# Mirrored token pairs in a fused FFT and MLP kernel: shared first layer in row tiles, maxima on VectorE, output sums on GpSimd, mirrored rows loaded by SyncE

**Chip, cores, metric.** One core of one Trainium2 chip. The metric is device time in microseconds (us) of one execution, lower is better. A profiled execution's *span* (first to last instruction) is about 2 us shorter than its time.

## The reference, cut to what matters

```python
# x: (8, 3136, 256) float32; U: (3136, 32); V: (32, 3136); w_ch1: (256, 1024); w_ch2: (1024, 256)
X  = np.fft.fft(np.fft.fft(x, axis=1), axis=2).real          # over the sequence, then over the features
h  = X.transpose(0, 2, 1) @ U @ V                            # low-rank mixing along the sequence
u  = X + h.transpose(0, 2, 1)
out = u + np.maximum(u @ w_ch1, 0.0) @ w_ch2                 # a two-layer MLP per token, with its residual
```

The 3136 tokens are treated as 49 "lines" of 64. The real part of the transform has a symmetry: token k and its mirror share the even half of the transformed row and have opposite odd halves. The kernel before uses it for the transform; the change uses it for the MLP too.

## The kernel before: the parts that matter

Batches are handled in four pairs. While one pair goes through the MLP, the rows of the next pair are loaded, folded and transformed by work placed between the MLP's slots. A chunk load, and the folds that use it:

```python
def load_pair_chunk(p, c):
    ...
    nc.sync.dma_start(out=ck.xa[:, 0:4, :], in_=x_pn[r0:r0 + PR, 4 * c + 1:4 * c + 5, :])      # PR = 98 rows
    ...
    nc.gpsimd.indirect_dma_start(                                                              # mirrored rows
        out=ck.xb.rearrange("p l d -> p (l d)"), out_offset=None, in_=x_g,
        in_offset=bass.IndirectOffsetOnAxis(ap=idx[:, 8 * p + c:8 * p + c + 1], axis=0))

def fold_d(yb, src, l0, l1):                         # after GpSimd has added xa and the reversed xb into y
    o, i = yb[:, l0:l1, :], src[:, l0:l1, :]
    nc.vector.tensor_tensor(o[:, :, 1:128], i[:, :, 1:128], i[:, :, 255:128:-1], op=AL.add)
    nc.vector.tensor_tensor(o[:, :, 129:256], i[:, :, 1:128], i[:, :, 255:128:-1], op=AL.subtract)
    nc.vector.tensor_copy(o[:, :, 0:129:128], i[:, :, 0:129:128])
```

The MLP: TensorE at full height, relu on ScalarE, output sums on VectorE, stores on SyncE.

```python
def mlp1(ch, jp):
    ...
    for i in range(2):
        ...
        for blk in range(2):
            nc.tensor.matmul(ps[:, i, 0:n], (W1p if ch.sg > 0 else W1m)[jp // 2][:, blk, j],
                             q[:, blk, c0:c0 + n], start=(blk == 0), stop=(blk == 1))
    nc.scalar.activation(ch.h[:, 2 * jp:2 * jp + 2, 0:n], ps[:, :, 0:n], AF.Relu)

def mlp2(ch, t, last=False):
    ...
    for j in range(JT):                              # JT = 8
        nc.tensor.matmul(ps, ch.h[:, j, t * P:(t + 1) * P], W2[:, j, :], ...)
        if j < 2:
            nc.tensor.matmul(ps[:, j], q[:, j, tk], (Bp if ch.sg > 0 else Bm)[:, j], ...)       # residual
    ...
    def drain():
        ...
        nc.scalar.copy(om[:, 0:n], ch.po[:, 0:n, 1])
        nc.vector.tensor_tensor(ob[:, 0:n, 0:P], ch.po[:, 0:n, 0], om[:, 0:n], op=AL.add)
        nc.vector.tensor_tensor(ob[:, 0:n, P:D], ch.po[:, 0:n, 0], om[:, 0:n], op=AL.subtract)
        ...                                          # nc.sync.dma_start of each half of ob
```

Of the kernel before, what the change touches and what calls it, by code (L numbers as in the profile page):

```python
# [22 lines left out]
def kernel(  # L23
# [21 lines left out]
    x_g = x.rearrange("b (n1 g l) d -> (b n1 g) (l d)", g=16, l=4)  # L45

    cpool = ctx.enter_context(tc.tile_pool(name="cpool", bufs=1))
    xpool = ctx.enter_context(tc.tile_pool(name="xpool", bufs=4))
# [3 lines left out]
    qpool = [ctx.enter_context(tc.tile_pool(name="qpool0", bufs=1)), None]  # L52
# [4 lines left out]
    T = cpool.tile([P, NK1, P], BF16)  # L57
# [3 lines left out]
    W1m = [cpool.tile([P, 2, 512], BF16, name=f"W1m{c}") for c in range(2)]  # L61
    W2 = cpool.tile([P, JT, D], BF16)
    Bp = cpool.tile([P, 2, P], FP16)
    Bm = cpool.tile([P, 2, P], FP16)
    tes = [cpool.tile([P, D], BF16, name=f"te_{b}") for b in range(2)]
    idx = cpool.tile([PR, 8 * NP], I32)
# [22 lines left out]
    def load_pair_chunk(p, c):  # L89

        ck = Obj()
        ck.c = c
        r0 = p * PR
        ck.xa = xpool.tile([PR, 5, D], FP32, tag="xa", name="xa")
        ck.xb = xpool.tile([PR, 4, D], FP32, tag="xb", name="xb")
        nc.sync.dma_start(out=ck.xa[:, 0:4, :], in_=x_pn[r0:r0 + PR, 4 * c + 1:4 * c + 5, :])
        if c == 7:
            nc.sync.dma_start(out=ck.xa[:, 4, :], in_=x_pn[r0:r0 + PR, 0, :])
        nc.gpsimd.indirect_dma_start(  # L99
            out=ck.xb.rearrange("p l d -> p (l d)"), out_offset=None, in_=x_g,  # L100
            in_offset=bass.IndirectOffsetOnAxis(ap=idx[:, 8 * p + c:8 * p + c + 1], axis=0))
        return ck

    def load_single(b):
# [10 lines left out]
        if b == 0:  # L115
            first.q = qpool[0].tile([P, 2, 6272], BF16, tag="q", name="q")
            xl = first.q[0:1].rearrange("p a j -> p (a j)")[:, 0:32 * D].rearrange("p (l d) -> p l d", d=D)
            nc.gpsimd.dma_start(out=xl, in_=x_pn[r0 + L:r0 + N1, 0:32, :])
        rows(33, 1, X[1:2 * L:2, 0:31, :])
        if b == 0:  # L120
            yield
            nc.sync.dma_start(out=X[PR - 2:PR - 1, 31::-1, :], in_=xl)
            yield
        else:
            nc.gpsimd.dma_start(out=X[PR - 2:PR - 1, 31::-1, :], in_=x_pn[r0 + L:r0 + N1, 0:32, :])
            yield
# [5 lines left out]
    def fold_d(yb, src, l0, l1):  # L132
# [3 lines left out]
        nc.vector.tensor_copy(o[:, :, 0:129:128], i[:, :, 0:129:128])  # L136
# [19 lines left out]
    class Pair:  # L156
        def __init__(self, p):
            self.p, self.z, self.q = p, None, None
# [10 lines left out]
    def s1_steps(pr, evac):  # L169
# [5 lines left out]
        def step(g):  # L175
            yb, l = pr.chunks[g // 2].yb, 2 * (g % 2)
            ps = psd.tile([P, 2, D], FP32, tag="ps", name="ps")
            if g == 15:
                parts = [(ps[:, 0], yb[:, 4], 1), (ps[:, 0], yb[:, 3], 2), (ps[:, 1], yb[:, 2], 0)]
            else:  # L180
                parts = [(ps[:], yb[:, l:l + 2], 0)]
# [6 lines left out]
            evac(z[:, 31::-31, :] if g == 15 else z[:, 30 - 2 * g:28 - 2 * g:-1, :] if g < 14 else z[:, 2:0:-1, :], ps[:])  # L188
            if g % 4 == 3:
                lo = max(30 - 2 * g - 1, 0)  # L190
                hi = 37 - 2 * g
                nc.scalar.dma_start(out=zdp[:, lo:hi, :], in_=z[:, lo:hi, :])
                if g == 15:
                    nc.scalar.dma_start(out=zdp[:, 31, :], in_=z[:, 31, :])
# [4 lines left out]
    def line32(b, ps=None, start=True):  # L199
        ps = ps if ps is not None else psd.tile([P, 2, D], FP32, tag="ps", name="ps32")  # L200
# [59 lines left out]
    def turn(pr, b, parts, engines=(nc.sync,)):  # L260
        g = gpool.tile([P, NK1, D], BF16, tag=f"g{b}", name="g")
        src = zd[pr.p % 2, b].rearrange("k cn d -> cn k d")
        for i, (k0, k1) in enumerate(parts):
            engines[i % len(engines)].dma_start(out=g[0:64, k0:k1], in_=src[:, k0:k1, :])
        pr.g[b] = g

    def te_out(pr, b, ps, c0, s0, spread):
        te = tes[b]
        nc.vector.tensor_copy(te[64:96, 0:129], ps[c0:c0 + 32, 0, 0:129])
        nc.vector.tensor_copy(te[96:128, 129:256], ps[s0:s0 + 32, 0, 129:256])  # L270
        spread(pr.g[b], te)

    def te_steps(pr, spread):
# [4 lines left out]
        def step(lo, hi):  # L278
            if lo == 0:
                st.ps = psd.tile([P, 2, D], FP32, tag="ps", name="teps")  # L280
# [5 lines left out]
            if hi == 32:  # L286
                for b in range(2):
                    te_out(pr, b, st.ps, 32 * b, 64 + 32 * b, spread)

        for lo, hi in [(0, 20), (20, 32)]:  # L290
            yield lambda lo=lo, hi=hi: step(lo, hi)

    def te_single(pr, b, spread, ps=None):

        ps = ps or psd.tile([P, 2, D], FP32, tag="ps", name="teps")
# [4 lines left out]
        te_out(pr, b, ps, 0, 32, spread)  # L300

    def spread(parts):
        def run(g, te):
            src = te[64:128].bitcast(I32)
            for eng, k0, k1 in parts:
                eng.tensor_copy(g[64:128, k0:k1].bitcast(I32), src.unsqueeze(1).to_broadcast([64, k1 - k0, D // 2]))  # L306
        return run

    def two(row, a, b, n):

        v = row[:, a:a + n]
        return bass.AP(row.tensor, v.offset, [list(v.ap[0]), [b - a, 2], [1, n]])

    def s3_steps(pr, b, evac):

        if pr.q is None:
            pr.q = qpool[pr.p % 2].tile([P, 2, 6272], BF16, tag="q", name="q")

        def mm(o, k1, blk, st, rows=P, low=None):
            lt = low[:, blk::2] if low is not None else pr.g[b][0:rows, k1, blk::2]  # L320
            r = T[0:rows, k1, 0:64] if k1 == 0 else T[0:rows, k1, :].rearrange("p (s j) -> p s j", s=2)
            nc.tensor.matmul(o, lt, r, start=st, stop=True, skip_group_check=True)  # L322

        def lines(ps, g, blk, rows, low=None):
            for u in range(4):
                us = slice(u * 64, (u + 1) * 64)
                mm(ps[:, 0, us] if 4 * g + u == 0 else ps[:, :, us], 4 * g + u, blk, u == 0 and low is None, rows, low)

        def step(g, blk):
            ps = psd.tile([P, 2, 256], FP32, tag="ps", name="ps")  # L330
            lines(ps, g, blk, P)
            move(ps, g, blk, evac)

        def move_part(ps, g, blk, evac, part):
            lo = 64 if part and g == 0 else 0
            c0 = 3200 + b * 1536 + (4 * g - 1) * 64 if part else b * 1600 + 4 * g * 64
            evac(pr.q[:, blk, c0 + lo:c0 + 256], ps[:, part, lo:256])

        def move(ps, g, blk, evac):
            if g == 0:  # L340
                move_part(ps, g, blk, evac, 0)
                move_part(ps, g, blk, evac, 1)
            else:
                k0 = 4 * g
                evac(two(pr.q[:, blk, :], b * 1600 + k0 * 64, 3200 + b * 1536 + (k0 - 1) * 64, 256), ps[:])

        def last():
            ps = psd.tile([P, 2, 2, 64], FP32, tag="ps", name="ps")
            k1 = NK1 - 1
            for blk in range(2):  # L350
                mm(ps[:, blk], k1, blk, blk == 0)
            for blk in range(2):
                evac(two(pr.q[:, blk, :], b * 1600 + k1 * 64, 3200 + b * 1536 + (k1 - 1) * 64, 64), ps[:, blk])

        yield lines, move_part
        for g in range(6):
            for blk in range(2):
                yield lambda g=g, blk=blk: step(g, blk)
        yield last


    def pair_chunks(p):

        res = []
        plus = [(2 * p + b, k1) for b in range(2) for k1 in range(NK1)]
        minus = [(2 * p + b, N1 - k1) for b in range(2) for k1 in range(1, NK1)]
        for sg, us, lo, hi, base in [(1, plus, 0, 24, 0), (-1, minus, 0, 24, 3200),
                                     (1, plus, 24, 50, 0), (-1, minus, 24, 48, 3200)]:
            for i in range(lo, hi, 8):
                ch = Obj()  # L370
                ch.p, ch.sg, ch.c0, ch.units = p, sg, base + 64 * i, us[i:min(i + 8, hi)]
                res.append(ch)
        return res

    def mlp1(ch, jp):
        q, c0, n = ch.pr.q, ch.c0, 64 * len(ch.units)
        if jp == 0:
            ch.h = hpool.tile([P, JT, 512], BF16, tag="h", name="hT")
        ps = psh.tile([P, 2, 512], FP32, tag="h", name="hps")
        for i in range(2):  # L380
            j = slice((2 * (jp % 2) + i) * P, (2 * (jp % 2) + i + 1) * P)
            for blk in range(2):
                nc.tensor.matmul(ps[:, i, 0:n], (W1p if ch.sg > 0 else W1m)[jp // 2][:, blk, j], q[:, blk, c0:c0 + n],  # L383
                                 start=(blk == 0), stop=(blk == 1))
        nc.scalar.activation(ch.h[:, 2 * jp:2 * jp + 2, 0:n], ps[:, :, 0:n], AF.Relu)  # L385

    def mlp2(ch, t, last=False):
        q, nt = ch.pr.q, len(ch.units) // 2
        if t % 2 == 0 or last:
            ch.po = pso.tile([P, 2, 2, P], FP32, tag="o", name="ops")  # L390
        ps = ch.po[:, 0 if last else t % 2]
        tk = slice(ch.c0 + t * P, ch.c0 + (t + 1) * P)
        for j in range(JT):
            nc.tensor.matmul(ps, ch.h[:, j, t * P:(t + 1) * P], W2[:, j, :],  # L394
# [475 lines left out]
```

## Time and profile before

| | before |
|---|---|
| median of 3 runs (lowest to highest) | 453.54 us (451.29 to 454.5) |
| span of the profiled run, mean granted TensorE clock | 449.6 us, 1.00 |
| busy: TensorE, ScalarE, VectorE, GpSimd | 95%, 65%, 50%, 32% |

The prediction below shows the busy shares, the last chain, the stretches and single instructions. The page's slices: each digit is a fortieth of the span, TensorE's busy share in tenths (9 is 90% or more).

```profile
PE   3889997999999999999999999999999999999995
...
PEclk9999999999999999999999999999999999999999
```

TensorE is full from the eighth slice on, and in this run its clock is never reduced while it works (other runs of the same kernel list a mean of 0.990 to 1.00). From the groups of instructions (count, then busy us and mean ns, then idle time before; the waits list us in total, times, longest): the folding add on VectorE.

```profile
L134 DVE TENSOR_TENSOR yb<-y 98x508 bf16<-98x508 f32 (+1 forms) x24 | 21.1, 879 | 0.1
```

### The profile page before, as it was taken

How to read it: one execution, taken by the hardware profiler on the slowest of the kernel's cores; microseconds unless marked ns; L12 is line 12 of the kernel's file. 1: busy time of each engine (PE TensorE's matmuls, PEld its weight loads, DVE VectorE, ACT ScalarE, POOL GpSimd, SP SyncE). 2: the span in 40 equal slices, each digit the busy share in tenths (PEclk: the TensorE clock that was granted, in tenths of full speed). 3: DMA queues.
4: the chain of work that ended last, by engine and by line, in shares of the span. 5: the costliest groups of instructions: out<-in, count | busy, mean ns of one | idle time of the engine just before them, and what ended most of it. 6: DMA issues, size and time to landing. Idle time of an engine off the chain costs nothing.

```text
span 449.6 us, 10536 instructions
## 1 busy us (share of the span) xinstructions
PE 426.6 (95%) x4158; PEld 308.7 (69%) x4221; DVE 224.6 (50%) x541; ACT 290.3 (65%) x402; POOL 142.6 (32%) x180
## 2 busy tenths in 40 slices
PE   3889997999999999999999999999999999999995
PEld 1756665776777777767867777777867777667764
DVE  7873686874344466373354467363354344222222
ACT  5886754676565567777465667777466655666662
POOL 7465455851330545550510545360500000000000
PEclk9999999999999999999999999999999999999999
DMA  8749753875592657863772647773662222222323
GB/s 149 159 138 168 211 162 109 254 181 176 162 231 66 171 137 214 235 207 96 171 195 62 171 113 238 223 200 101 165 141 66 71 65 66 72 72 74 85 54 93
DMA packets 59761, 64.34 MB, mean 143 GB/s; under 512 B 12950, under 2 KB 52672, under 8 KB 59552
## 3 DMA queue, kind: packets, MB, share of 16 engines
q1 hardware_dynamic: 50000, 42.68, 36.8%
q0 software_dynamic: 7232, 14.30, 13.5%
q10 hardware_dynamic: 2480, 6.69, 4.0%
q8 instruction: 33, 0.54, 0.5%
q14 instruction: 16, 0.13, 0.1%
HBM read 34.62 MB, written 32.19 MB: 149 GB/s over the span
## 4 chain that ended last, share of the span: by engine, by line
PE 84%; DVE 5%; DMA 3%; issue 3%; POOL 2%; ACT 1%; SPq 1%; DVEq 0%; ACTq 0%; POOLq 0%
PE ops L394 35%; PE hps L383 35%; PE ps L322 5%; PE ops L397 4%; PE ps L185 2%; DMA out_dram<-ob 2%; PE teps L284 1%; DMA w_f<-in_moe_w_ch_dram 1%; SPq L412 1%; DVE g L76 1%; ACT hT L385 1%; PE w1ps L679 1%; DVE q L76 0%; DVE ta L447 0%; DVE ob L407 0%
## 5 line engine op out<-in xcount | busy, mean ns | idle before, releaser
L385 ACT ACTIVATE hT<-hps 128x1024 bf16<-128x1024 f32 (+1 forms) x208 | 202.6, 976 | 109.6 <-PE hps L383 100.9
L394 PE MATMUL ops<-W,hT 128*128 128x256 bf16 x1568 | 224.7, 273 | 1.2 <-DVE ob L408 1.0
L394 PEld LDWEIGHTS <-hT 128*128 128x128 bf16 x1568 | 145.1, 98 | 35.0 <-DVE ob L408 0.8
L76 DVE CAST q<-ps 128x512 bf16<-128x512 f32 (+3 forms) x121 | 65.2, 560 | 83.8 <-PE ps L322 80.1
L383 PE MATMUL hps<-q,W1p 128*128 128x512 bf16 (+1 forms) x420 | 103.2, 355 | 2.6 <-DVE q L76 0.5
L407 DVE TENSOR_TENSOR ob<-ops,om 128x256 f32<-128x256 f32 (+1 forms) x102 | 41.8, 410 | 117.7 <-ACT om L406 116.3
L383 PE MATMUL hps<-q,W1m 128*128 128x512 bf16 x351 | 95.7, 379 | 2.1 <-ACT hT L385 0.5
L144 POOL TENSOR_TENSOR y<-xa,xb 98x510 f32<-98x510 f32 (+1 forms) x48 | 60.9, 1289 | 108.5 <-DMA xa<-in_x_dram 84.2
L383 PEld LDWEIGHTS <-W1p 128*128 128x128 bf16 x448 | 40.3, 98 | 27.3 <-issue 2.2
L383 PEld LDWEIGHTS <-W1m 128*128 128x128 bf16 x384 | 35.3, 98 | 26.5 <-issue 1.4
L397 PEld LDWEIGHTS <-q 128*128 128x128 bf16 x392 | 38.3, 98 | 21.6 <-issue 0.9
L406 ACT COPY om<-ops 128x256 f32<-128x256 f32 (+1 forms) x102 | 37.3, 366 | 14.4 <-PE ops L394 7.8
L306 POOL COPY g<-te 64x1024 int32<-64x1024 int32 (+1 forms) x23 | 24.9, 1122 | 56.3 <-DVE te L270 51.7
L408 DVE TENSOR_TENSOR ob<-ops,om 128x256 f32<-128x256 f32 (+1 forms) x102 | 41.2, 404 | 0.0
L73 ACT CAST z<-ps 128x512 bf16<-128x512 f32 x48 | 28.2, 587 | 17.2 <-PE ps L185 16.4
L397 PE MATMUL ops<-Bp,q 128*128 128x128 f16 x200 | 38.4, 219 | 0.0
L322 PE MATMUL ps<-T,g 128*128 128x128 bf16 (+3 forms) x400 | 36.9, 218 | 0.5 <-ACT q L73 0.3
L397 PE MATMUL ops<-Bm,q 128*128 128x128 f16 x192 | 36.9, 219 | 0.0
L322 PEld LDWEIGHTS <-g 128*128 128x128 bf16 (+1 forms) x400 | 29.4, 98 | 5.0 <-issue 0.6
L99 POOL DMA_INDIRECT xb<-in_x_dram,idx x24 | 25.1, 1044 | 5.4 <-issue 4.5
L134 DVE TENSOR_TENSOR yb<-y 98x508 bf16<-98x508 f32 (+1 forms) x24 | 21.1, 879 | 0.1
L76 DVE COPY g<-zt 32x400 bf16<-32x400 bf16 (+3 forms) x45 | 17.2, 383 | 6.3 <-ACT zt L73 5.7
(136 smaller groups left out, 208.1 us busy)
## 6 DMA issues: line engine op xcount, KB each, us to landing
out_dram<-ob SPq DMA_DIRECT2D x389, 64.0 KB
xa<-in_x_dram SPq DMA_DIRECT2D x24, 392.0 KB
zturn<-z ACTq DMA_DIRECT2D x9, 512.0 KB
g<-zturn SPq DMA_DIRECT2D x3, 800.0 KB
g<-zturn SPq DMA_DIRECT2D x3, 544.0 KB
X<-in_x_dram POOLq DMA_DIRECT2D x4, 384.0 KB, 7.7
X<-in_x_dram POOLq DMA_DIRECT2D x2, 744.0 KB
zturn<-z ACTq DMA_DIRECT2D x3, 448.0 KB
```

The lines of the kernel that those rows point to most:

```text
L73: nc.scalar.copy(o, i)
L76: nc.vector.tensor_copy(o, i)
L99: nc.gpsimd.indirect_dma_start(out=ck.xb.rearrange("p l d -> p (l d)"), out_offset=None, in_=x_g, in_offset=bass.IndirectOffsetOnAxis(ap=i ...
L144: nc.gpsimd.tensor_tensor(ck.y[:, l0:l1, 1:256], ck.xa[:, l0:l1, 1:256], rb[:, l0:l1, 255:0:-1], op=AL.add)
L322: nc.tensor.matmul(o, lt, r, start=st, stop=True, skip_group_check=True)
L383: nc.tensor.matmul(ps[:, i, 0:n], (W1p if ch.sg > 0 else W1m)[jp // 2][:, blk, j], q[:, blk, c0:c0 + n], start=(blk == 0), stop=(blk == 1))
L385: nc.scalar.activation(ch.h[:, 2 * jp:2 * jp + 2, 0:n], ps[:, :, 0:n], AF.Relu)
L394: nc.tensor.matmul(ps, ch.h[:, j, t * P:(t + 1) * P], W2[:, j, :], start=(j == 0 and (t % 2 == 0 or last)), stop=(j == JT - 1), skip_group ...
L397: nc.tensor.matmul(ps[:, j], q[:, j, tk], (Bp if ch.sg > 0 else Bm)[:, j], start=False, stop=False, skip_group_check=True)
L406: nc.scalar.copy(om[:, 0:n], ch.po[:, 0:n, 1])
L407: nc.vector.tensor_tensor(ob[:, 0:n, 0:P], ch.po[:, 0:n, 0], om[:, 0:n], op=AL.add)
L408: nc.vector.tensor_tensor(ob[:, 0:n, P:D], ch.po[:, 0:n, 0], om[:, 0:n], op=AL.subtract)
```

## The change

The intent is to let the first layer be computed once for the two tokens of a mirrored pair. With a and b the even and odd parts, relu(a+b) = max(a, -b) + b and relu(a-b) = max(a, b) - b; the b terms are linear and go through the product W1·W2 into the residual weights. Even and odd parts lie on 64 rows each, so that TensorE works on two row tiles at a time. ScalarE copies the odd part out of PSUM, VectorE forms both maxima with the even part read from PSUM, GpSimd forms the output sums, `te` (the transformed tokens times U, the inner part of the low-rank mixing) is no longer spread over the rows of `g` (the transformed lines from which the MLP's input is made), and the mirrored rows are loaded by SyncE in two groups of 49. The diff, cut to its core:

```diff
-        nc.gpsimd.indirect_dma_start(
-            out=ck.xb.rearrange("p l d -> p (l d)"), out_offset=None, in_=x_g,
-            in_offset=bass.IndirectOffsetOnAxis(ap=idx[:, 8 * p + c:8 * p + c + 1], axis=0))
+        r = 2 * p * N1 * 16 + 48 * 16 + 15 - c
+        nc.sync.dma_start(out=ck.xb.rearrange("p l d -> p (l d)"),
+                          in_=bass.AP(x.tensor, x.offset + r * 4 * D, [[N1 * 64 * D, 2], [-64 * D, N1], [1, 4 * D]]))
 ... (fold_d)
-        nc.vector.tensor_copy(o[:, :, 0:129:128], i[:, :, 0:129:128])
+        nc.scalar.copy(o[:, :, 0:129:128], i[:, :, 0:129:128])
 ... (first layer)
-        nc.scalar.activation(ch.h[:, 2 * jp:2 * jp + 2, 0:n], ps[:, :, 0:n], AF.Relu)
+                for s in range(2):                                   # row tiles 0..63 (even) and 64..127 (odd)
+                    lt = W1z[64:P, ja] if s and blk == 0 else W1p[c][64 * s:64 * s + 64, blk, jc]
+                    nc.tensor.matmul(o[s], lt, q[64 * s:64 * s + 64, blk, c0:c0 + w], ...)
+ ...                                                                 # the te part: TE by VZ, 33 rows per tile
+        ab = apool.tile([P, 512], BF16, tag="ab", bufs=3, name="ab")
+        nc.scalar.copy(ab[:], ps[:, 1])
+        ...
+        nc.vector.scalar_tensor_tensor(h[:, 1], b, -1.0, a, op0=AL.mult, op1=AL.max)
+            nc.vector.tensor_tensor(flip[0][:, :, ::-1], flip[1], flip[2], op=AL.max)
 ... (second layer: two phases; phase 1 waits for a no-op on ScalarE that follows phase 0)
+            for j in range(JT):
+                for s, op, half in sides:
+                    mm = nc.tensor.matmul(op, ch.h[rows[half], s, j, t * P:(t + 1) * P], W2[rows[half], j, :], ...)
+                    if ha and j == 0 and half == 0:
+                        tc.add_manual_dep(mm.ins, st.turn.ins.name, sync, reason="bank turn")
+            if ha == 0:
+                st.turn = nc.scalar.nop()
 ... (drain; eng is GpSimd except at the very end)
+                nc.scalar.copy(om, po)
+            eng.tensor_tensor(ob[:, 0:n, 0:P], a, om[:, :, 1], op=AL.add)
+            eng.tensor_tensor(ob[:, 0:n, P:D], a, om[:, :, 1], op=AL.subtract)
 ... (te row of each group of lines; the turn of z through DRAM moves from ScalarE's queue to SyncE's)
+            nc.sync.dma_start(out=zr, in_=q[64:65, 0, c0:c0 + 512])
-                nc.scalar.dma_start(out=zdp[:, lo:hi, :], in_=z[:, lo:hi, :])
+                nc.sync.dma_start(out=zdp[:, lo:hi, :], in_=z[:, lo:hi, :])
 ... (placing of the next pair's steps)
-                for o, f in [(0, load), (4, fn), (7, fd), (9, s1[2 * c]), (10, s1[2 * c + 1])]:
+                for o, f in [(0, load), (2, fn), (4, fd), (5, s1[2 * c]), (5, s1[2 * c + 1])]:
```

A slot of the kernel before is a quarter of a chunk of 512 tokens, one of the changed kernel half a chunk of 256 mirrored pairs, so that "slot" in the last lines has different lengths (1.8 and 3.5 us of TensorE work). The cut leaves out that the loaded rows have three buffers instead of four; b1 below keeps four.

## The prediction, on record before anything of the change was built

> **What bounds the kernel now.** I read the shares of the page first, then the chain of work that ended last, then the waits, then busy time by stretches and single instructions of TensorE in order of time.
>
> ```profile
> PE 426.6 (95%) x4158; PEld 308.7 (69%) x4221; DVE 224.6 (50%) x541; ACT 290.3 (65%) x402; POOL 142.6 (32%) x180
> ...
> PE 84%; DVE 5%; DMA 3%; issue 3%; POOL 2%; ACT 1%; SPq 1%; DVEq 0%; ACTq 0%; POOLq 0%
> ```
>
> TensorE is busy for 95% and is 84% of the last chain. No other engine passes 65%. The stretches (columns: length, then PE, PEld, DVE, ACT, POOL busy) say that this is a full engine, not one that waits in pieces:
>
> ```profile
> 70.00:80.00 10.00, 7.69 (x100) 5.50 (x101) 6.91 (x21) 4.23 (x7) 5.32 (x6) 1.00 0.36 90
> ...
> 130.00:140.00 10.00, 9.95 (x98) 7.67 (x97) 6.21 (x13) 5.87 (x7) 0.00 (x0) 1.00 0.42 125
> 200.00:210.00 10.00, 9.95 (x77) 7.04 (x77) 4.03 (x12) 7.80 (x11) 0.00 (x0) 1.00 0.40 120
> ...
> 440.00:450.00 10.00, 4.46 (x43) 3.38 (x40) 2.71 (x10) 1.75 (x6) 0.00 (x0) 0.98 0.38 98
> ```
>
> From 80 us to the end PE holds 9.6 to 9.95 of every 10 us. Losses lie only in the first 28 us (preparation), at 55 to 85 us (about 3 us, in the first pair of batches), and some 5 us at the end. The hole near 70 us is one link of the chain in time:
>
> ```profile
> 68.30 1.22 POOL y L144
> 69.52 0.20 POOL y L145
> 69.72 4.59 issue
> 74.31 1.15 POOL g L306
> ```
>
> GpSimd sits 4.59 us ahead of the copy that spreads `te` over the rows of `g`; PE matmuls on `g` follow it. So the time can fall by much only if TensorE gets less to do.
>
> To count that work I need the spacing of matmuls, not their busy durations, which overlap. The timeline gives it:
>
> ```profile
> 25.20 1.01 PE L322 MATMUL ps<-T,g 64*128 64x64 bf16 x16
> ...
> 114.97 1.32 PE L284 MATMUL teps<-z,UZ 128*64 128x129 bf16 x40
> 116.23 0.40 PE L383 MATMUL hps<-q,W1p 128*128 128x128 bf16 x4
> ...
> 116.79 0.82 PE L394 MATMUL ops<-W,hT 128*128 128x256 bf16 x6
> ```
>
> The last line: six matmuls of 256 columns in 0.82 us, the last lasting 0.27, so 0.55/5 = **0.109 us per 256 columns**; 512 columns take 0.216, 128 take 0.055, single starts show. The first line has 64 contraction rows and costs (1.01-0.22)/15 = 0.053: half the rows alone save nothing. The second has two column tiles: 20 pairs of about 128 columns in 1.10 us, 0.055 per *pair*, so two tiles truly run side by side. It also shows a price: its first start is 0.20 us after the preceding one instead of 0.109, and the first start after it is 0.15 late instead of 0.055, so **about 0.1 us to enter and 0.1 us to leave** a tiling.
>
> [...] 98x510 takes GpSimd 1.317 us, 98x508 takes VectorE 0.926 and 0.857.
>
> **The change, part by part.** Tokens k and 49-k share the even and odd half of the transformed row. The first layer computes both halves once (a and b, 64 contraction rows each, in two row tiles) and forms relu(a+b)=max(a,-b)+b and relu(a-b)=max(a,b)-b; the b terms go linearly through W1·W2 into the residual. One slot is 256 tokens.
>
> *TensorE.* First layer before, per 512 tokens: 16 x 0.216 = 3.46 us; second with its residual 4 x (8 x 0.109 + 2 x 0.055) = 3.93; together 7.38, and 12.25 such per pair of batches = 90.5 us. After, per slot: first layer two times 6 row pairs (four of weights, two of the separate te part) = 1.31; second layer two phases of 8 row pairs and 2 residual pairs = 20 x 0.109 = 2.18; sum 3.49, and 24 slots = 83.7, plus a short chunk of the zero lines of about 2.7: 86.4. Lines (L322): before 100 matmuls x 0.055 = 5.5; after the same number with 64 columns, in row pairs, at most 50 x 0.055 = 2.7. New: te through W1 (8 x 0.216 = 1.7) and through the residual (0.7). Sum: 90.5+5.5 = 96.0 against 91.5, **4.5 us less per pair of batches**. But all is row-tiled now, so the full-height pieces (s1 in eight slots, te) each enter and leave: about 11 more round trips of 0.2 = 2.3 us where a next pair is prepared (three of four). TensorE work: -(3 x 2.2 + 4) = **about -10 us**.
>
> *ScalarE.* Leaves: 202.6 (relu) + 37.3 + 28.2 + 3.9 of 290.3, so 18 stays. Comes: odd halves 192+8 copies 128x512 at 0.587 (z's row) = 117; reversed q 48 x 0.58 = 28; output copies 96 x 0.59 = 57; lines 24 x 1.03 = 25; z 23; te, tables, fold copies 28. About 296 us: same load.
>
> *VectorE.* Leaves: q casts 65 and sums 83, some small: about 60 stays, folding 43 of it. Comes: two maxima per 128x512, at 0.155 + 512 x 1.03 ns = 0.685 (slope from 0.289 at 128 columns to 0.420 at 256, L407): 400 x 0.685 = 274. About **335 us, from 50% to 75% or more**, 82 us of the 98 of a folding pair.
>
> *GpSimd.* Leaves: spread 25, indirect issues 25. Comes: 192 sums of 128x256 at about 0.83 (0.34 at 98x4, 1.317 at 98x510) = 159, small folds 8: about 260 us. No longer idle, not the bound. Loads of mirrored rows move to SyncE's queue: the same bytes, and DMA is at a third; I count nothing.
>
> *Waits.* Before, separate PSUM buffers let PE run ahead. Now four share one ring, and phase 1 must wait for the no-op that stands in ScalarE's line behind the odd copy, in even slots also the reversed q (0.58), and the evacuations of the slot before. In an even slot after a 1.0 us evacuation: lines end 0.55, first layer 1.20, phase 0 2.29, next layer 2.94 us, when PE wants phase 1; ScalarE: evacuation 0.75 to 1.75, output copy to 2.34, odd copy to 2.93, q to 3.51, no-op. PE loses 0.6 us. Some 8 such slots and a few doubled ones: up to 6.5 us per pair, 25 in all.
>
> *Sum.* 453.5 - 10 (matmuls) - 5 (the te hole and its neighbours; no spread is left) + 3 (W1·W2, more tables and evacuations in the first slots) + 6 (waits, a quarter of the worst since the steps seem placed against them) = **447 us**. The quarter is a choice, not a measurement.
>
> **Rivals.** *A, the waits hit in full*: 25 us instead of 6, and VectorE, which in the first pair also has the `g<-zt` copies (17 us over two batches), makes PE stop there: about 466. For it: VectorE over 80% with bursts (a fold is 1.8 us in a 4 us slot), in-order queues, four buffers. Against: ScalarE keeps its 65% and catches up in light slots. *B, the waits are hidden and lines and switches cost less*: tile switches overlap, row-tiled weight loads too; 4.5 x 4 saved, 5 from the hole, no waits: about 430. For it: a schedule this elaborate looks placed by traces. *C, row tiles do not overlap*: a slot's 40 pairs-members run singly, near 7 us instead of 3.5; over 700 us. Nothing in the trace supports it, as column tiles overlap. I give it 2%.
>
> **Range and chances.** Between B and A: 428 to 470. The 2% marks are 444.5 and 462.6. My middle lies just inside "same", but work of TensorE does go and the hole is real, so faster gets 0.42, same 0.34, slower 0.24.
>
> **What would show it.** Right: hT maxima on VectorE near 0.69 us each, VectorE near 335 us; row pairs 0 to 5 ns apart and 0.109 us per pair; PE still the top of the chain with its slices at 8 to 9 rather than a flat 9; waits of PE on ScalarE (no-op, evacuations) of 5 to 10 us in total, and on VectorE maxima a few us. Wrong: a pair spacing well over 0.109 (weight loads in the way), VectorE or GpSimd in the chain for more than a tenth (rival A), or PE flat at 9.9 with a span near 430 (B).

## More of the kernel before

```profile
POOL y L144 <- DMA xa<-in_x_dram: 84.2, 10, 24.7
...
POOL y L144 <- DMA xb<-in_x_dram,idx: 1.4, 1, 1.4
```

GpSimd waited 84 us for `xa`, and no wait of TensorE goes back to that; `xb` was the last to come only once, for 1.4 us. (A wait for several things is put down to the one that came last.)

## The result, and the profile after

| | before | after |
|---|---|---|
| median of 4 runs (lowest to highest) | 452.68 us (451.29 to 454.5) | 616.42 us (612.87 to 617.76) |
| ratio to before, 95% interval | | 1.360 (1.352 to 1.368) |
| span of the profiled run, mean granted clock | 449.6 us, 1.00 | 614.3 us, 0.875 |

Ratios here and below are the mean time of one kernel's fast runs over that of the other's of the same rounds, so not quite the ratio of the medians quoted. The outputs are correct. The change is 36% slower, far outside the range of 428 to 470 us; "slower" was given 0.24.

The page of the changed kernel: busy time, slices, chain.

```profile
PE 485.0 (79%) x8159; PEld 384.2 (63%) x8159; DVE 356.6 (58%) x592; ACT 279.0 (45%) x505; POOL 249.4 (41%) x342
...
PE   4788798294869798886584979878677498999995
...
PEclk9788997686978798797795879988869589999998
...
PE 15%; DVE 3%; ACT 1%; issue 1%; DMA 0%; DVEq 0%; ACTq 0%; POOL 0%
```

Three readings. No engine is a new bound: VectorE holds 58%, the others less. TensorE has holes all through the first 80% of the span and is full only in the last slices, the last pair, in which no next pair is prepared. And **its clock is reduced** in more than half of the slices, which the profile before does not show once. (The chain is of little use here: it goes back only to 482 us of 614.)

**A budget.** I split both spans into TensorE's tail after its last instruction, its idle time, and its busy time, and divided the busy time by the granted clock: stretches on record at half clock are counted half as work, the other half as loss.

| us | before | after | difference |
|---|---|---|---|
| TensorE idle | 18.2 | 122.7 | +104.5 |
| lost to half clock while busy | 0 | 54.8 | +54.8 |
| TensorE work at full clock | 426.6 | 430.2 | +3.6 |
| tail | 4.9 | 6.5 | +1.6 |

(18.2 + 0 + 426.6 + 4.9 = 449.7, and 122.7 + 54.8 + 430.2 + 6.5 = 614.2.) 159 of the 165 us are idle time and half clock. The row of work needs care: a matmul of 256 columns that is followed at once by another adds 0.109 us, but the last one before a pause shows its whole 0.27 us. Pauses over 0.1 us number 16 before and 94 after; an estimate from the matmul records puts what they add to the row at 2.7 and 14.4 us, so that without it the work fell by some 8 us, from 423.9 to 415.9.

**Where it lies in time.** By the first instruction of each pair's MLP:

| length, us | start | pair 0 | pair 1 | pair 2 | pair 3 |
|---|---|---|---|---|---|
| before | 28.0 | 114.0 | 102.1 | 102.2 | 103.4 |
| after | 33.3 | 168.4 | 153.5 | 154.0 | 105.0 |

The last pair, beside which no next pair is prepared, is 1.6 us longer than before. Nearly all, 158 of 165 us, is lost where the next pair is loaded, folded and transformed meanwhile.

**One pause followed back.** Waits of the changed kernel, for the engines that belong to it:

```profile
POOL y L151 <- DMA xb<-in_x_dram: 184.1, 22, 15.0
...
ACT yb L143 <- POOL y L152: 76.9, 18, 11.2
...
DVE yb L141 <- POOL y L151: 62.6, 18, 9.7
...
PE ops L480 <- ACTq L492: 41.3, 11, 8.7
...
PE hps L432 <- DMA VZ<-q: 27.1, 5, 11.6
```

GpSimd, which had waited 86 us for `xa` and `xb` together, now waits 184 us for `xb`, and this time others wait for GpSimd. The timeline (start, busy time; in brackets the idle time before and what ended it) has one such wait from end to end:

```profile
480.55 1.95 POOL L151 TENSOR_TENSOR y<-xa,xb 98x510 f32<-98x510 f32 x2 [15.00 <-DMA xb<-in_x_dram]
...
482.53 3.27 DVE L141 TENSOR_TENSOR yb<-y 98x381 bf16<-98x381 f32 x1 [9.73 <-POOL y L151]
482.69 0.22 ACT L143 CAST yb<-y 98x6 bf16<-98x6 f32 x1 [11.21 <-POOL y L152]
...
482.98 1.89 PE L480 MATMUL ops<-W,hT 64*128 64x256 bf16 x16 [8.66 <-ACTq L492]
```

`xb` lands at 480.5. GpSimd has stood 15 us at its addition; the fold follows; ScalarE has stood 11 us at its small fold copy (L143); behind that copy in its line, at 482.90, stands the no-op between the two phases of the second layer, and TensorE resumes 0.3 us after the copy has begun, 8.66 us idle. The first thing to explain is why `xb` is late, although the same bytes are loaded.

**What the pauses do to the clock.** Stretches of 5 us (busy time of PE, PEld, DVE, ACT, POOL; granted clock; DMA share; GB/s):

```profile
325.00:330.00 5.00, 0.74 (x8) 0.56 (x10) 1.18 (x1) 1.02 (x4) 3.16 (x5) 0.50 0.12 38
330.00:335.00 5.00, 3.29 (x25) 1.71 (x21) 5.00 (x6) 0.73 (x2) 3.67 (x5) 0.50 0.34 78
335.00:340.00 5.00, 4.49 (x46) 3.08 (x47) 3.56 (x6) 2.18 (x4) 1.41 (x2) 0.50 0.38 84
340.00:345.00 5.00, 5.00 (x113) 4.27 (x111) 1.29 (x2) 1.70 (x5) 0.00 (x0) 0.90 0.47 159
```

TensorE is nearly idle from 325 to 330; the clock is at 0.5 and stays there to about 341, long after TensorE is working again: 46 matmuls in 5 us at half clock, 113 at nearly full. All 12 pauses of this trace that are over 2.5 us were followed by half clock, for 3.4 to 17.1 us, so each of these was paid twice.

**What the prediction had right.** From the groups:

```profile
L438 DVE SCALAR_TENSOR_TENSOR hT<-ab,hps 128x512 bf16<-128x512 bf16 x200 | 136.6, 683 | 172.3 <-ACT ab L435 172.2
...
L441 DVE TENSOR_TENSOR hT<-hps,ab 128x512 bf16<-128x512 f32 x192 | 130.8, 681 | 0.0
...
L141 DVE TENSOR_TENSOR yb<-y 98x508 bf16<-98x508 f32 (+1 forms) x24 | 33.8, 1409 | 62.7 <-POOL y L151 62.6
```

The maxima take 0.68 us each, as worked out; the folding add went from 0.88 to 1.41 us, which was not. And from the timeline of the undisturbed last pair:

```profile
565.98 1.03 PE L480 MATMUL ops<-W,hT 64*128 64x256 bf16 x16
...
567.73 1.03 PE L480 MATMUL ops<-W,hT 64*128 64x256 bf16 x16
```

16 matmuls (8 row pairs) in 1.03 us, the members of a pair 0 to 3 ns apart, 0.109 per pair in the mean; phases 1.75 us apart, so 3.50 us a slot, against 3.49 predicted.

### The profile page after: what moved, and what is told of

The parts are those of the page before. It is cut to its first block, busy times and chain, and to the rows that moved or that the text cites. A ratio compares the mean times of both kernels' runs of the same rounds, so it can differ in the third digit from the quotient of the medians.

```text
span 614.3 us, 19104 instructions
## 1 busy us (share of the span) xinstructions
PE 485.0 (79%) x8159; PEld 384.2 (63%) x8159; DVE 356.6 (58%) x592; ACT 279.0 (45%) x505; POOL 249.4 (41%) x342
## 3 DMA queue, kind: packets, MB, share of 16 engines
q8 instruction: 63, 1.03, 0.7%
## 5 line engine op out<-in xcount | busy, mean ns | idle before, releaser
L480 PE MATMUL ops<-W,hT 64*128 64x256 bf16 x3072 | 224.7, 287 | 48.4 <-ACTq L492 41.3
L438 DVE SCALAR_TENSOR_TENSOR hT<-ab,hps 128x512 bf16<-128x512 bf16 x200 | 136.6, 683 | 172.3 <-ACT ab L435 172.2
L480 PEld LDWEIGHTS <-hT 64*128 64x128 bf16 x3072 | 158.9, 100 | 85.7 <-ACTq L492 44.6
L435 ACT CAST ab<-hps 128x512 bf16<-128x512 f32 x200 | 117.0, 590 | 127.1 <-PE hps L432 107.1
L425 PE MATMUL hps<-q,W1p 64*128 64x256 bf16 (+1 forms) x1248 | 131.3, 281 | 13.0 <-DVE hT L441 11.2
L522 POOL TENSOR_TENSOR ob<-om 128x256 f32<-128x256 f32 (+1 forms) x97 | 78.0, 804 | 142.5 <-ACT om L521 121.3
L441 DVE TENSOR_TENSOR hT<-hps,ab 128x512 bf16<-128x512 f32 x192 | 130.8, 681 | 0.0
L425 PE MATMUL hps<-q,W1z 64*128 64x256 bf16 (+1 forms) x416 | 106.3, 282 | 0.0
L432 PE MATMUL hps<-VZ,TE 33*128 33x256 bf16 (+1 forms) x896 | 84.5, 273 | 27.4 <-DMA VZ<-q 27.1
L425 PEld LDWEIGHTS <-W1p 64*128 64x128 bf16 x1248 | 72.9, 99 | 31.0 <-DVE hT L441 19.4
L523 POOL TENSOR_TENSOR ob<-om 128x256 f32<-128x256 f32 (+1 forms) x97 | 78.2, 806 | 0.0
L143 ACT CAST yb<-y 98x8 bf16<-98x8 f32 (+1 forms) x24 | 5.5, 227 | 76.9 <-POOL y L152 76.9
```

The costliest lines, as they stand in the source:

```text
L425: nc.tensor.matmul(o[s], lt, q[64 * s:64 * s + 64, blk, c0:c0 + w], start=(i == 0 and blk == 0), stop=True, skip_group_check=True)
L432: nc.tensor.matmul(ps[:, s, i * w + a:i * w + a + n], TE[ch.p % 2][b][64 * s:64 * s + 33, ja], VZ[64 * s:64 * s + 33, b, v:v + n], start=F ...
L435: nc.scalar.copy(ab[:], ps[:, 1])
L438: nc.vector.scalar_tensor_tensor(h[:, 1], b, -1.0, a, op0=AL.mult, op1=AL.max)
L441: nc.vector.tensor_tensor(flip[0][:, :, ::-1], flip[1], flip[2], op=AL.max)
L480: mm = nc.tensor.matmul(op, ch.h[rows[half], s, j, t * P:(t + 1) * P], W2[rows[half], j, :], start=(ha == 0 and j == 0), stop=False, skip_ ...
```

## The experiments

Thirteen kernels ran. Times are medians. Each is told with what was written before it ran.

| run | what it is | us | ratio to before | idle | lost to half clock |
|---|---|---|---|---|---|
| after | the change | 616.4 | 1.360 | 122.7 | 54.8 |
| e2 | after, mirrored rows by GpSimd again | 521.6 | 1.154 | 67.9 | 14.7 |
| b1 | before, mirrored rows by SyncE | 565.7 | 1.249 | 108.5 | 26.8 |
| e7 | after, one list of 98 rows (wrong rows) | 520.8 | 1.143 | 62.5 | 21.5 |
| e8 | after, 2 x 49 rows ascending (wrong rows) | 619.4 | one run | 129.4 | 50.6 |
| e3 | after, small fold copy on VectorE | 613.5 | 1.356 | 129.3 | 46.9 |
| e5 | after, loads further ahead | 594.5 | 1.313 | 117.1 | 39.7 |
| p1, p2 | before, with nine short / long pauses | 461.9, 522.7 | 1.022, 1.158 | 26.0, 70.7 | 0, 17.5 |
| e4 | e2, te row on ScalarE's queue | 522.0 | 1.147 | 62.8 | 18.8 |
| e6 | e4, one fold add on GpSimd | 518.2 | 1.132 | 61.1 | 15.8 |
| e9 | e6, half of turned-row copies on ScalarE | 511.1 | 1.128 | 55.2 | 16.7 |
| e10 | e9, output copies first in a slot | 516.1 | 1.146 | 62.5 | 12.6 |
| x1 | e2, one maximum only (wrong result) | 497.9 | 1.103 | 47.7 | 12.7 |

(Idle and half clock are of the profiled run, by the budget above. Medians are over all runs, ratios over fast runs: e4 and e7 had one slow run each, e6 two, whose two fast ones took 511.1 and 517.5 us. e6's profiled run was slow. The state of e8's one run is unknown, but it lies 99 us above e7, and no two runs of one kernel here differ by more than 13 us.)

### Is it the load of the mirrored rows?

Theory T1: the new load is late, and everything else follows from it. Rival T2: the no-op chain and the balance of engines. First the load alone was undone (e2), the load alone was put into the kernel before (b1), the copy that passes the wait on to ScalarE was put back on VectorE (e3), and the load was given more lead (e5).

**e2.** The changed kernel with the indirect load of before:

```diff
-        nc.sync.dma_start(out=ck.xb..., in_=bass.AP(x.tensor, ..., [[N1 * 64 * D, 2], [-64 * D, N1], [1, 4 * D]]))
+        nc.gpsimd.indirect_dma_start(out=ck.xb..., in_=x_g, in_offset=bass.IndirectOffsetOnAxis(ap=idx[...], axis=0))
```

> Undoes one part: the mirrored x rows come again by GpSimd's indirect DMA, as before the change; all else as after the change. Theory T1 (the two-row-group form of SyncE's load runs on few DMA engines and lands late; the fold's small copy, which stands in ScalarE's line, waits for it, and with it the no-op that TensorE needs; TensorE's pauses then halve its clock): TensorE waits on the no-op fall from 41 us to under 10, GpSimd's wait on the mirrored rows from 184 us to under 60, mean clock at least 0.96, time 440 to 490. Rival T2 (the ring of four PSUM buffers, VectorE at 80% and in-order queues make the pauses whatever the load does): time above 550, clock still below 0.92.

Measured 521.6 us, 1.154 (1.147 to 1.160): correct, and 95 us below the changed kernel, between the two expectations. GpSimd's wait for `xb`:

```profile
POOL y L153 <- DMA xb<-in_x_dram,idx: 6.8, 5, 2.6
```

From 184 to 6.8 us. By the budget the load costs the changed kernel 54.8 us of idle time and 40.1 us of half clock. Some 68 us remain without it.

**b1.** The same load, alone, in the kernel before:

```diff
-        nc.gpsimd.indirect_dma_start(...)
+        r = 2 * p * N1 * 16 + 48 * 16 + 15 - c
+        nc.sync.dma_start(out=ck.xb..., in_=bass.AP(x.tensor, x.offset + r * 4 * D, [[N1 * 64 * D, 2], [-64 * D, N1], [1, 4 * D]]))
```

> The kernel before, with only the mirrored x rows loaded by SyncE in the two-row-group form. It folds four of its shorter slots (about 7.4 us) after the load, its VectorE works on the fold 13 us after it, and its ScalarE and PSUM buffers do not hang on the fold. T1: GpSimd waits more on the rows, TensorE hardly: 0 to 4% slower (453 to 472), clock 0.98 or more. If the slow load by itself is enough to stop any such kernel: above 500.

Measured 565.7 us, 1.249 (1.244 to 1.254). My expectation that the tuned kernel before would absorb it missed entirely: this one line costs it 114 us, with the same pauses (idle +90) and half clock (27), no row tiles and no no-op. Waits of this kernel, then those of SyncE's queue:

```profile
POOL y L144 <- DMA xb<-in_x_dram: 264.5, 24, 35.4
...
PE hps L383 <- ACT hT L385: 43.1, 7, 10.0
ACT om L406 <- DMA out_dram<-ob: 42.1, 5, 11.4
```
```profile
SPq L412 <- DMA xb<-in_x_dram: 104.3, 20, 7.5
```

L412 are the output stores. SyncE's queue stands 104 us at `xb` before it issues them, output buffers come free late, ScalarE's output copy (`om`) waits, and TensorE waits for the relu behind that copy. Why a store waits for a load can be read from the changed kernel's trace: each of its 19 such waits (86 us) is that of the eighth DMA on SyncE after the load, and it waits on the semaphore that the load had waited on too. In that trace SyncE's 523 DMAs take eight semaphores in turn (65 or 66 each), and in these 19 cases seven more DMAs were issued after the load before the queue stood until it landed. The change hurts through whatever stands in line behind a late DMA; the no-op is only one of the ways.

**e3.** The small fold copy, which had moved to ScalarE, back on VectorE:

```diff
-        nc.scalar.copy(o[:, :, 0:129:128], i[:, :, 0:129:128])
+        nc.vector.tensor_copy(o[:, :, 0:129:128], i[:, :, 0:129:128])
```

> Undoes one part: the fold's small copy (98x8) is done by VectorE again, so that ScalarE's line waits no more for GpSimd's fold; the load stays slow. If ScalarE's blocked line is what matters, the no-op wait goes and the time falls to under 520. If the late rows block VectorE just as well (its folds stand in the same line as the maxima), the waits only move from the no-op to the maxima and the time stays within 5% of 616. I expect the latter, 585 to 616. T2: no change.

Measured 613.5 us, 1.356: no gain, as expected. TensorE's largest wait is now

```profile
PE s L194 <- DVE yb L143: 43.1, 13, 9.0
```

43 us, where the no-op had 41. The wait only changed its name: the folds stand in VectorE's line as well.

**e5.** Loads four slots ahead of their fold instead of two, all later steps two slots later, and the loads set slightly closer together (gaps of 1.5 and 2.0 slots instead of 1.75 and 2.3):

```diff
-                for o, f in [(0, load), (2, fn), (4, fd), (5, s1[2 * c]), (5, s1[2 * c + 1])]:
+                for o, f in [(0, load), (4, fn), (6, fd), (7, s1[2 * c]), (7, s1[2 * c + 1])]:
```

> Keeps SyncE's load and everything else, but asks for each pair of x rows four slots ahead of the fold instead of two (some 14 us instead of 7), and folds a slot or two later in relation to the load. T1: a load that lands 9 to 13 us after its issue is then mostly in time; time 460 to 520, clock 0.94 or more, no-op wait under 15 us. T2: above 570.

Measured 594.5 us, 1.313. Missed: more lead gives back 22 us of 95. GpSimd's wait for `xb` fell from 184 to 108 us, but SyncE's queue stood 111 us at `xb` (81 in the changed kernel), and TensorE's waits for the te rows grew from 27 to 38 us. So it is not just latency that could be hidden by asking earlier: the stores behind the load are held up all the same (in this trace too, every one of the 23 waits for `xb` in SyncE's queue is on the semaphore that the DMA eight before it had taken).

### Why is the load slow? e7 and e8

The new load has an outermost dimension of 2 and a negative step. Two kernels, wrong (they read other rows), tell one from the other:

```diff
 # e7: one list of 98 ascending rows
-                          in_=bass.AP(x.tensor, x.offset + r * 4 * D, [[N1 * 64 * D, 2], [-64 * D, N1], [1, 4 * D]]))
+                          in_=bass.AP(x.tensor, x.offset + (r - 48 * 16) * 4 * D, [[64 * D, 2 * N1], [1, 4 * D]]))
 # e8: two groups of 49, ascending
+                          in_=bass.AP(x.tensor, x.offset + (r - 48 * 16 - 2 * N1 * 16) * 4 * D, [[2 * N1 * 64 * D, 2], [64 * D, N1], [1, 4 * D]]))
```

> Wrong result on purpose: as after the change, the rows loaded by SyncE at the same moments and with the same bytes, but in ascending order, which lets the access be one list of 98 rows in place of two groups of 49. If the form (an outermost dimension of 2) is what makes the load slow, this run behaves like the indirect one: 505 to 535 us, clock 0.95 or more[...]. If SyncE's queue itself (stores ahead of the load, one issuer for all) makes it late, it stays at 590 to 620.

> Wrong result on purpose: two groups of 49 rows again, but in ascending order (from other batches[...]). If the outermost 2 is the cause, as slow as after the change: 600 to 625 us. If the negative step is the cause, as fast as the 98-row run: 505 to 535.

e7 took 520.8 us, as fast as the indirect load; e8 619.4 us in its one run, as slow as the change. The waits of e7, then of e8:

```profile
POOL y L151 <- DMA xb<-in_x_dram: 21.0, 8, 4.6
```
```profile
POOL y L151 <- DMA xb<-in_x_dram: 190.0, 23, 14.9
```

Both ascend; they differ in the outermost dimension and in which (wrong) rows they read. **The outermost 2 is the cause, not the reversal and not SyncE.** How many of the 16 engines carry the load is an estimate, since the packet records do not name the engine. A packet of 4096 bytes takes 0.159 us in the changed kernel (median), so one engine with one packet at a time would start 3.1 of them in 0.5 us, and two 6.3. In the changed kernel 350 half-microseconds have 5 to 8 such packets, 7.3 us for each of the 24 loads, and hold 38% of all packets of that size; e8 has 351 such halves, e7 11. For instance 6 to 7 packets started in each half from 269.5 to 277.0 us, while `xa` of the same load had come with 12 to 37 in each.

What that means for the load, as an estimate from these numbers: 98 packets x 0.159 / 2 = 7.8 us for a load, 187 us for 24, on two engines that would each also carry a sixteenth of all other traffic, about 236 us (42.3% of 16 engines' 614.3 us, less the 374 us of `xb`, by 16). Together that is 423 us on two engines, against the 450 us of the span before, while the mean share of all 16 is 0.55 in the profile before and 0.42 in that after. (The estimate takes the load as lying on two engines and the other traffic as evenly spread.)

A direct repair on SyncE is not among the runs.

### What do pauses cost through the clock? p1 and p2

Theory, from the changed kernel's trace: a pause of some us halves the clock for a while after it (the halved stretches that end within that trace last 3.4 us or a multiple of it, up to 17.1). To see it without the change, nine pauses were put into the last pair of the kernel *before*: a matmul, a VectorE copy of its result, n small GpSimd operations on it, a matmul that needs them; n = 1 in p1 and 12 in p2.

```diff
+    def pause():
+        ps = bank_d("pause")
+        nc.tensor.matmul(ps[:, 0, 0:64], pz, pz[:, 0:64], start=True, stop=True)
+        nc.vector.tensor_copy(pz2, ps[:, 0, 0:64])
+        for _ in range(12):                                      # p1: range(1)
+            nc.gpsimd.tensor_scalar(pz2, pz2, 1.0, None, op0=AL.mult)
+        nc.tensor.matmul(ps[:, 1, 0:64], pz, pz2, start=True, stop=True)
+        ...
+        for k in range(5, 46, 5):
+            if p == NP - 1: at[k].append(pause)
```

> The kernel before, with nine artificial pauses of TensorE in the last pair of batches: a small matmul, a copy by VectorE, one small operation of GpSimd, and a small matmul that needs it. I expect pauses of 0.8 to 1.2 us each. If a pause costs only its own length: 7 to 11 us more than 452, clock 1.0. If any pause halves TensorE's clock for one window of 3.4 us (the lengths of the halved stretches in the trace are multiples of 3.4): another 1.7 us each, 22 to 27 us more in all. From the trace after the change (windows before a halving are busy for less than about half) I expect no halving here.

> The same nine pauses with twelve small operations of GpSimd in a row instead of one: 2.8 to 4 us each. Pause alone: 25 to 36 us more than 452. With halved clock after it, at least one window of 3.4 us at half speed, 1.7 us lost each: 40 to 52 us more, mean clock 0.93 to 0.96. This measures by itself the part of the loss that my prediction had no term for.

p1 took 461.9 us, 1.022 (1.019 to 1.026) to the kernel before: pauses of 0.77 us, clock 1.00 throughout. p2 took 522.7 us: its pauses came out at 5.72 us, longer than I had meant, and each of the nine was followed by a stretch of half clock of 3.4 or 6.8 us. One of them in the timeline:

```profile
374.86 0.19 PE L784 MATMUL pause<-UZ 128*128 128x64 bf16 x1
380.77 0.21 PE L788 MATMUL pause<-UZ 128*128 128x64 bf16 x1 [5.72 <-POOL UZ L787]
...
383.12 1.49 PE L394 MATMUL ops<-W,hT 128*128 128x256 bf16 x6
...
386.76 0.82 PE L394 MATMUL ops<-W,hT 128*128 128x256 bf16 x6
```

The same six matmuls take 1.49 us at 383 and 0.82 us at 387. p2 is 60.8 us slower than p1, its pauses are 44.5 us longer in sum (9 x 4.95), so 16.3 us, **1.8 us for each pause, are the clock's**; the budget, apart from that, has 17.5. The changed kernel has 54.8 us of it, e2 14.7.

Shorter pauses were followed by half clock too, where there were several. In the four traces looked through (after, b1, e4, p2) every halving within the MLP followed 3.4 us in which TensorE was busy at most 0.56 of the time (0.49 in the changed kernel), nearly always under 0.5; in the preparation of the changed kernel two followed 0.59 and 0.77. Before the halving at 419.5 us of the changed kernel TensorE was busy 0.48 of 3.4 us, and its longest pause there was 0.71 us. The nine pauses of 0.77 us that stood alone (p1) were followed by none. What sets the halving off is not shown beyond that.

### What is left without the load

e2 is still 68 us over the kernel before (span 517.4 against 449.6): idle +49.7, half clock +14.7, work +1.8, tail +1.5. By pairs it has 142.4, 120.9, 118.3 and 105.4 us against 114.0, 102.1, 102.2 and 103.4: **28 of it in the first pair**, 35 in the two others with a next pair, and 2 each in the last and before the first. The waits of TensorE in e2:

```profile
PE hps L434 <- DMA VZ<-q: 13.7, 3, 6.3
PE hps L427 <- DVE hT L443: 10.1, 12, 2.3
...
PE tk L317 <- DVE G L877: 5.0, 2, 4.5
```

Te rows through SyncE's queue, VectorE's maxima, the product W1·W2 for the first use. Of the no-op, 41 us in the changed kernel, there is no wait left. Five kernels tried these, each on top of e2 or of the one before it.

**e4**, the te row from ScalarE's queue:

```diff
-            nc.sync.dma_start(out=zr, in_=q[64:65, 0, c0:c0 + 512])
+            nc.scalar.dma_start(out=zr, in_=q[64:65, 0, c0:c0 + 512])
```

> The indirect load, and the small copy of a line of q into VZ is started from ScalarE's queue instead of SyncE's, where it stands behind output stores that wait for GpSimd. In the run with the indirect load TensorE waited 13.7 us for that row (5 to 6 us at each pair's start) and the clock halved after it. If that wait is one cause of what is left: TensorE's wait on VZ under 3 us, time 15 to 30 us lower than 521, so 490 to 506. If another wait takes its place: 510 to 525.

522.0 us, 1.147: no gain. The wait for VZ is gone from the list, and another is there, which is not among e2's:

```profile
PE ops L482 <- ACTq L494: 7.3, 5, 3.2
```

**e6**, e4 with the first of the two fold operations as `nc.gpsimd.tensor_tensor` in place of `nc.vector.tensor_tensor`:

> As the run with the row copy on ScalarE's queue, and in addition one of the two folding additions goes from VectorE to GpSimd. After the change VectorE's folding additions take 1.41 us instead of 0.88 and stand in front of the maxima. If VectorE's bursts are the other cause, TensorE's waits on the maxima (about 20 us) halve and the time falls by another 8 to 20 us. If GpSimd, now about 300 us busy, then delays the folds or the output sums: same or slower by up to 15 us.

518.2 us, 1.132 (1.114 to 1.150): not told apart from e4.

**e9**, e6 with every second of the first pair's turned-row copies on ScalarE:

```diff
-                quarter_rows(g, st.zt, 4 * r - 4, [copy_dve] * 8)
+                quarter_rows(g, st.zt, 4 * r - 4, [copy_dve, copy_act] * 4)
```

> As the run with one fold addition on GpSimd (518 us), and the copies of turned rows of the first pair (8 per step, all VectorE) go half to ScalarE. If VectorE's load in the first pair is what makes its pauses (4.2 us once, 1 to 2 us several times): 5 to 15 us less, 503 to 513. If ScalarE's line then delays the odd halves as much: 514 to 525.

511.1 us, 1.128 (1.123 to 1.134). Of the correct variants of the change this has the lowest median, 10 us below e2, and it is 13% over the kernel before; it is not told apart from e6, so what the turned-row copies gave is not shown.

**e10**, e9 with `m.drain(...)`, the output copy and sums, ahead of the slot's evacuations instead of after them:

> As the one before, and in each slot the output copy of the second layer stands ahead of the evacuations of the slot's other steps in ScalarE's line (it stood behind them). My rival A counted pauses from this order: a 1.0 us evacuation ahead of the output copy, the odd copy and the no-op. If the order matters, TensorE's small waits on maxima and evacuations shrink: another 5 to 15 us less. If the pauses come from VectorE alone: within 3 us of the one before.

516.1 us, 1.146: no gain, rather 5 us worse; TensorE's wait at the no-op went from 7.3 to 14.7 us.

**x1**, e2 with one of the two maxima replaced by a write of zeros (wrong), to price VectorE's load:

```diff
-            nc.vector.tensor_tensor(flip[0][:, :, ::-1], flip[1], flip[2], op=AL.max)
+            nc.vector.memset(h[:, 0].rearrange("p i n -> p (i n)").bitcast(FP32), 0.0)
```

> Wrong result on purpose, to relieve VectorE: the run with the indirect load (521 us), but the second of the two maxima is replaced by writing zeros to the same place (about 0.3 us instead of 0.68, and no read of PSUM), some 70 us less of VectorE's work and a shorter hold of each PSUM buffer; TensorE's instructions are the same. If what is left after the load is mended (about 50 us more pauses than before, 15 us of halved clock) comes from VectorE's load, the time falls to 470 to 490, with gaps of TensorE at 35 us or less. If it comes from the no-op and ScalarE's order, the late rows of VZ or the start of the first pair alone, it stays at 505 to 525.

497.9 us, 1.103 (1.099 to 1.107), span 493.2: between its expectations. VectorE is busy 55 us less and the span is 24 us shorter, 20 of it idle time of TensorE (in e2 TensorE had waited 23 us at this maximum, L443). **About a third of the rest goes with the second maximum**: VectorE's load, or the PSUM buffer that it holds until it is done, which x1 does not separate. 44 us stay. What makes up those 44 us was not separated further. The waits named point to the te rows and the turned rows, both of which come through SyncE's queue (11.4 and 6.7 us of TensorE's waits in x1), and to the product W1·W2 (5 us); e4 shows that taking one such wait away need not give its time back.

## Why the prediction was wrong, point by point

1. **"Loads of mirrored rows move to SyncE's queue: the same bytes, and DMA is at a third; I count nothing."** This step failed and is the larger part: e2 is 95 us below the changed kernel, e7 likewise, e8 not, and b1 adds 114 us to the kernel before. The bytes are the same, but by the estimate above their packets come at the rate of two engines of sixteen; I looked at the average share of 16 engines instead of the shape of the access pattern. I had named three rivals and none had a DMA in it.
2. **No term for the clock.** The sum added waits at their own length. The profile of the kernel before shows a clock of 1.00 throughout, so nothing in its profile said it, but "what would the clock do if TensorE paused" could have been asked. It measured 54.8 us, 40 of them through the load. It also makes a wait dearer than it looks: p2's pauses of 5.7 us cost 1.8 us each on top.
3. **"TensorE work: about -10 us"** measured +3.6 by the budget, but most of the miss is in how the budget counts. The mechanism was right: row pairs run together at 0.109 us and a slot is 3.50 against 3.49. Without the whole last matmul before each pause, the estimate given below the budget, the work fell by about 8 us, by 2.7 and 2.6 in pairs 1 and 2 where I had 2.2. One mis-sized term can be named: te through the first layer and the residual, with the product W1·W2, came to about 14 us, for which I had 9.6 (2.4 a pair of batches) and a part of the "+3". So about what the change was to save on TensorE seems to have been saved, and was lost many times over in pauses.
4. **"+ 6 (waits, a quarter of the worst since the steps seem placed against them)".** Half of the mechanism, which is rival A's, was right: with the load mended (e2), TensorE stands 24 us at VectorE's maxima. The other half, TensorE at the no-op behind ScalarE's line, was not: that wait is gone in e2, and its 41 us in the changed kernel came from the late rows; it is back at 7 us in e4 and e9. The size was off as well: e2 has 50 us more idle time than the kernel before, twice rival A's full 25, and 15 us of half clock. The second maximum accounts for some 24 us of span (x1); whether the 5 us for the vanished spread of te came back can't be read, since pair 0, where they were, lost 28 us in e2. What the rest consists of stays open.
5. **Right:** the maxima, 0.68 us against 0.685; GpSimd 249 us against 260, ScalarE 279 against 296. VectorE is at 357 against 335: most of it the two folding operations, 1.41 and 1.10 us instead of 0.88 and 0.82, 19.5 us in sum. They now run beside more GpSimd work; that this is the cause was not tested.
6. **Readings to put right.** That the column pairs run side by side stands: in the line quoted their members start 0 to 14 ns apart. "Half the rows alone save nothing" does not follow from one line of 64 columns without a full-height one of 64 columns beside it. How far GpSimd lies behind VectorE differs with the work: the output sums take 0.80 us against 0.41 on VectorE before, the folding sizes that the prediction gives are only 1.4 and 1.5 apart.

The 0.24 for "slower" had rival A in mind; most of the 36% came from a line that I had not priced.

## What to carry to other kernels

Look at the outermost dimension of every DMA that a change adds or rewrites before counting its bytes: the load with an outermost 2 cost 95 to 114 us here (e2, b1), one list of 98 rows was as fast as the indirect load (e7), and more lead gave back less than a quarter (e5). Then ask what stands in line behind it, since here a store (b1), a small copy and a no-op (the changed kernel) in the same queue passed its lateness on to the bound engine, 43 and 41 us of TensorE's waits. And where TensorE is the bound, price a pause of a few microseconds at its length plus the half clock that may follow, 1.8 us for each of 5.7 us here (p2).
